# An order written out by hand for 2033 steps: its first three batches re-ordered, and the PSUM banks written down with it

## The chip, the cores and the metric

The kernel runs on one core of a Trainium2 chip. The metric is the device time of one execution in microseconds, as the median of several runs. A profile of one execution, taken by the hardware profiler, stands beside it.

## What is computed

Softmax attention with a one added to the sum of exponentials, and on its output a gate with a long convolution done by Fourier transform. Eight batches, twelve heads of 64, 448 positions, so a model width of 768.

```python
scores = q @ k.T / 8                       # 8 x 12 heads, 448 x 448
e = np.exp(scores - m)                     # m: the row's maximum
attn = e / (e.sum(-1) + np.exp(-m) + 1e-09)
x = heads_side_by_side(attn @ v)           # 8 x 448 x 768
x1, x2, x3 = split(x @ w_proj)             # 768 -> 3 x 768
conv = irfft(rfft(x2) * rfft(filter_fft))  # along the 448 positions
out = (x1 * conv * x3) @ w_out             # 768 -> 768, float32
```

## The kernel before

Two heads (a pair) are worked on together; `attention(i)` is one of the 48 pairs, and `dense(b)` the gate of one of the eight batches. All operations are written down as some 2033 steps by `add(engine, cost, ...)` of the class `Plan`: what a step needs and makes, which buffers it takes (`take`) and gives back (`give`). Some copies out of PSUM may go to either ScalarE (ACT) or VectorE (DVE); `FLIP` lists the numbers of the steps that swap engines.

`plan.ORDER` holds one key for each step. On each engine (TensorE, ACT, DVE, GpSimd called POOL, and SyncE called SP, which issues most transfers) the steps are sorted by it, and with `ORDER` set only the step at the head of each engine's list may start. So the order on an engine is fixed; a step whose operand is late holds up all that stands behind it on its engine. `Plan.run` plays the five lists against each other by modelled times, and in doing so chooses a PSUM bank for each step that takes one. The instructions are then written out in the order of that play, and on the chip they wait for each other by semaphores alone. The bank that a step got decides which earlier reader it must wait for.

PSUM has eight banks. Three kinds of user share them: "sc" (scores, pairs of banks), "op" (the output of a pair of heads, pairs of banks) and "hy" (all the dense part, single banks, at most five at once). The function `spots` chooses: the pair that has been free longest, or for "hy" a bank whose neighbour is taken, by preference.

How the batches flow:

- `staged(b)` loads q, k and v for batches 0 and 1, turns them with matmuls against the identity (L624, L637), and copies qT and kT out of PSUM (L486 on ACT, L488 on DVE). `loaded(b)` does it for later batches: loads by SP (L727 q, L747 k, L509 the rests) and by POOL (L754 v), casts on POOL (L733, L759, L771), and transposes by DMA (L694 qT, L705 kT).
- `more_tables` builds the Fourier tables: `mirror` is the matmul of L847, and `fr` is copied out by ACT (L854, L855).
- `attention(i)`: scores (L947, L952), exponentials on ACT (L966), the rest of an output (L977, 64-row tiles) and its main part (L997), the division (L1010 to L1012), and a DMA transpose of the result into xT (L1056). Before the second half of a pair may write its bank, a one-element step called `seen` (L987, `sinks`, on POOL for all pairs but batch 0's) waits for L977.
- `dense(b)`: sums and differences for the transform (`u`, `w`, `xf`, L1125 to L1134), the projection of x2 (L1175) with a copy out and a DMA transpose (L1188), the forward transform Z (L1223) with the filter (L1241), the gate matmuls G (L1273) with x1's copy and the product g (L1288), the inverse I (L1319), y (L1361), and the output projection (L1091). Its copy into `osb` (L486 or L488) is stored by SP (L1406). `osb` is a ring of three buffers.
- `wout_load` (L929) loads w_out by POOL's queue. It is needed by the first L1091.

The work of two or three batches overlaps: while TensorE does the scores of one batch, it does the dense part of the batch before.

An output tile's copy takes one of the three buffers, and its store gives it back:

```python
add("ACT", 0.38, w, ..., alt=None if keep else ("DVE", 0.47), need=[("O", b, st, ch)] + past("ACT"),
    make=[("os", b, st)] + [("os", b, st, ch)], take=held, give=[hy], keep=keep)
...
add("SP", 0.5, w, lambda: store(st), need=[("os", b, st)] + past("SP"), make=[("store", b, st)], give=held, ...)
```

Of the kernel before, what the change touches and what calls it, by code (L numbers as in the profile page):

```python
# [41 lines left out]
class Plan:  # L42
# [17 lines left out]
    FLIP = ()  # L60
    FETCH = (4.6, 256, 150)
# [14 lines left out]
    def __init__(self, rings):  # L76
        self.size = rings
        self.tasks = []
        self.banks = {}
        self.kept = []  # L80
        self.open = []

    def add(self, eng, cost, want, emit, need=(), make=(), take=(), give=(), dma=0.0, run=256, n=1, after=0.0, begun=(), late=0.0, turn=False, part=None, keep=False, port=False, mode=None, alt=None, mm=None):
        if alt:
            own = (eng, cost)
            (eng, cost), alt = (alt, own) if len(self.tasks) in self.FLIP else (own, alt)
            emit = lambda f=emit, e=eng: f(e)
        want = self.ORDER[len(self.tasks)] if self.ORDER else want + self.SHIFT.get(part, 0.0)
        self.tasks.append((want, len(self.tasks), eng, cost, emit, need, make, take, give, dma, after, run, n, begun, late, turn, keep, port or eng == "POOL" and not dma, mode or ("full" if eng == "PE" and not keep else None), alt, 2 * (mm or max(1, round(cost / 0.17)) if eng == "PE" and cost else 0)))

    def run(self):
# [79 lines left out]
        def spots(t):  # L171

            found, count = {}, {}
            for r, tok in t[7]:
# [47 lines left out]
        while any(queue.values()):  # L222
            moved = False
            for e in queue:
# [22 lines left out]
                if t[20]:  # L247
# [3 lines left out]
                    while edge <= fed + t[20]:  # L251
                        at = now + cost * (edge - fed) / t[20] + wait
# [1425 lines left out]
```

## Time and profile before

| | before |
|---|---|
| median of 3 runs | 373.16 us (373.08 to 374.23) |
| span of the profiled execution | 370.8 us |
| instructions | 10707 |
| TensorE (PE) busy | 356.4 us, 96% |
| VectorE (DVE) busy | 274.8 us, 74% |
| ScalarE (ACT) busy | 237.5 us, 64% |
| GpSimd (POOL) busy | 127.6 us, 34% |
| read from and written to HBM | 43.86 MB and 11.01 MB |

How to read it: the profile follows one execution, and its span goes from the first instruction to the last; the profiled execution has no time of its own beside its span, and the times of the runs are longer by what lies around it (373.16 - 370.8 = 2.36 us for the median). Busy time counts what an engine works; weight loads for TensorE (PEld) overlap its matmuls. A row of the timeline has its start, its duration, the engine, the line, the operation, the tiles out and in, and in brackets the idle time of the engine ahead of it with what ended that. SPq is SP's own queue of transfers to issue; the landing of a transfer comes later than its issue. A wait row has the engine and what waited, what it waited for, then the sum, the count and the longest, in us.

### The profile page before, as it was taken

What the parts mean: (1) busy time and instruction counts of PE and PEld (TensorE: products, weight loads), DVE (VectorE), ACT (ScalarE), POOL (GpSimd) and SP (SyncE); (2) the same over time, 40 slices, a digit from 0 to 9 for tenths busy, and PEclk for the clock granted to TensorE, in tenths of its full rate; (3) what the DMA queues carried; (4) which work ended last, traced back from release to release, by engine and by line L of the source; (5) the groups of instructions that cost most, each with busy time, mean ns of one, the idle gap of its engine ahead of it and who ended that gap; (6) DMA issues with size and microseconds to landing.
All of it is one profiled execution on the core that took longest, in us unless ns stands there. A gap on an engine that the chain in (4) does not pass through costs nothing. (4 is left out here: it accounts for less than half of the span.)

```text
span 370.8 us, 10707 instructions
## 1 busy us (share of the span) xinstructions
PE 356.4 (96%) x4300; PEld 211.8 (57%) x4300; DVE 274.8 (74%) x674; ACT 237.5 (64%) x379; POOL 127.6 (34%) x278
## 2 busy tenths in 40 slices
PE   7989999999999979999999999999999999999995
PEld 7666675554555545565555646665565655555552
DVE  5468659982789726897579977689459898779970
ACT  4999876756767548567565657867776561334343
POOL 9984251444625274265537523313100100000000
PEclk9999999999999999999999999999999999999999
DMA  9999999988999999999998799995830074125035
GB/s 169 194 191 204 207 207 205 206 169 160 168 242 156 229 214 208 235 242 192 206 182 202 166 245 192 262 208 122 171 72 1 7 196 89 42 45 170 4 129 172
DMA packets 133958, 61.93 MB, mean 167 GB/s; under 512 B 105165, under 2 KB 130704, under 8 KB 133904
## 3 DMA queue, kind: packets, MB, share of 16 engines
q1 hardware_dynamic: 111552, 48.71, 61.6%
q0 software_dynamic: 22112, 12.26, 25.4%
q8 instruction: 34, 0.56, 0.6%
q10 hardware_dynamic: 240, 0.23, 0.2%
q14 instruction: 20, 0.16, 0.2%
HBM read 43.86 MB, written 11.01 MB: 148 GB/s over the span
## 5 line engine op out<-in xcount | busy, mean ns | idle before, releaser
L966 ACT ACTIVATE e<-psum 128x896 bf16<-128x896 f32 x144 | 126.6, 920 | 40.8 <-PE psum L947 37.3
L1273 PE MATMUL psum<-xT,wproj_bf 128*128 128x448 bf16 x576 | 121.7, 353 | 0.1
L1273 PEld LDWEIGHTS <-wproj_bf 128*128 128x128 bf16 x576 | 53.4, 98 | 47.7 <-issue 5.0
L1091 PE MATMUL psum<-wout_bf,yT 128*128 128x384 bf16 x288 | 54.7, 326 | 0.8 <-DVE g L1288 0.4
L1175 PE MATMUL psum<-xf,wproj_bf 128*128 128x452 bf16 x252 | 53.9, 357 | 0.0
L947 PE MATMUL psum<-qT,kT 64*64 64x448 bf16 x576 | 45.4, 359 | 2.5 <-DVE g L1288 0.7
L997 PEld LDWEIGHTS <-e 128*128 128x128 bf16 x1152 | 42.0, 98 | 9.6 <-issue 5.2
L997 PE MATMUL psum<-vn,e 128*128 128x65 bf16 x1152 | 46.8, 194 | 0.0
L733 POOL CAST nat<-nat 112x512 bf16<-112x512 f32 x36 | 25.4, 708 | 44.7 <-DMA nat<-in_q_dram 41.8
L1241 DVE TENSOR_TENSOR t<-xs,hrs 113x768 bf16<-113x768 bf16 (+1 forms) x64 | 36.4, 578 | 2.9 <-ACT xs L486 2.3
L1288 DVE TENSOR_TENSOR g<-x,psum 128x448 bf16<-128x448 bf16 x48 | 29.2, 616 | 12.1 <-PE psum L1273 10.9
L1091 PEld LDWEIGHTS <-yT 128*128 128x128 bf16 x288 | 26.6, 98 | 19.9 <-issue 1.8
L1175 PEld LDWEIGHTS <-wproj_bf 128*128 128x128 bf16 x252 | 23.2, 96 | 22.2 <-issue 1.1
L486 ACT CAST x<-psum 128x448 bf16<-128x448 f32 (+1 forms) x39 | 20.4, 529 | 22.6 <-PE psum L1273 14.5
L759 POOL CAST nat<-nat 128x384 bf16<-128x384 f32 x36 | 21.5, 598 | 32.2 <-DMA nat<-in_k_dram 31.9
L486 ACT COPY osb<-psum 128x384 f32<-128x384 f32 x39 | 18.2, 486 | 20.1 <-PE psum L1091 15.9
L486 ACT CAST xs<-psum 113x384 bf16<-113x384 f32 (+1 forms) x41 | 19.2, 482 | 15.1 <-PE psum L1223 14.1
L1012 DVE TENSOR_TENSOR xb<-psum,den 128x896 bf16<-128x896 f32 x24 | 26.2, 1091 | 0.8
L486 ACT CAST cr<-psum 128x452 bf16<-128x452 f32 x35 | 18.0, 539 | 11.5 <-PE psum L1319 11.0
L947 PEld LDWEIGHTS <-kT 64*64 64x64 bf16 x576 | 15.6, 105 | 17.1 <-issue 12.9
L966 ACT ACTIVATE er<-psum 128x896 bf16<-128x896 f32 x24 | 22.2, 926 | 4.3 <-PE psum L952 3.5
L987 POOL MEMSET sinks<- 1x1 bf16 x18 | 1.6, 91 | 65.6 <-PE psum L977 65.6
(143 smaller groups left out, 501.3 us busy)
## 6 DMA issues: line engine op xcount, KB each, us to landing
nat<-in_q_dram SPq DMA_DIRECT2D x37, 224.0 KB, 3.8
out_dram<-osb SPq DMA_DIRECT2D x21, 384.0 KB, 3.5
nat<-in_k_dram SPq DMA_DIRECT2D x38, 192.0 KB, 3.9
nat<-in_v_dram POOLq DMA_DIRECT2D x15, 192.0 KB, 6.3
wproj_bf<-in_moe_w_proj_dram POOLq DMA_DIRECT2D x2, 1152.0 KB, 18.1
out_dram<-osb SPq DMA_DIRECT2D x12, 192.0 KB, 2.7
ks<-in_v_dram POOLq DMA_DIRECT2D x9, 192.0 KB, 4.9
rests<-in_k_dram SPq DMA_DIRECT2D x32, 48.0 KB, 4.3
```

The lines of the kernel that those rows point to most:

```text
L486: nc.scalar.copy(to, of)
L733: lambda hp=hp, qsrc=qsrc: nc.gpsimd.tensor_copy(qn[:, hp].rearrange("p j (u d) -> p u j d", u=2), qsrc.rearrange("p (u j d) -> p u j d", ...
L759: lambda hp=hp, sv=sv: nc.gpsimd.tensor_copy(kn[:, hp // 2, 3 * (hp % 2) + 1 : 3 * (hp % 2) + 4].rearrange("p j (u d) -> p u j d", u=2), sv),
L947: nc.tensor.matmul(sc[r, u, 0:S], kT[b % 2][c, hp // 2, 3 * turned + t, r], qT[b % 2][c, hp, :])
L966: nc.scalar.activation(to, of, AF.Exp, scale=SCALE)
L997: nc.tensor.matmul(out_bank(u)[:, n + 3 * turned, :], P["e"][1 + t][:, o : o + 128], vn[b % 2][:, hp, 4 * u + t, :], start=False, stop=tur ...
L1012: nc.vector.tensor_tensor(W["xb", b][:, hp // 2].rearrange("p s (u d) -> p u s d", u=2), op[:, :, :, 0:DH], rec[:].unsqueeze(3).to_broadca ...
L1091: nc.tensor.matmul(ops[:n, :DCH], y[:, dt, 0:n], wout_bf[:, dt, ch * DCH : (ch + 1) * DCH], start=(dt == 0), stop=(dt == NDT - 1),)
L1175: nc.tensor.matmul(pps, wproj_bf[:, kt, D + dt * 128 : D + (dt + 1) * 128], W["xf", b][:, :, kt, 0:FQ], start=(kt == 0), stop=(kt == NDT - 1),
L1241: nc.vector.tensor_tensor(t[:K], L["xs", par, ch][:K], h, op=ALU.mult)
L1273: nc.tensor.matmul(p[:, :S], wproj_bf[:, kt, 2 * part * D + dt * 128 : 2 * part * D + (dt + 1) * 128], xT()[:, kt, 0:S], start=(kt == 0), ...
L1288: nc.vector.tensor_tensor(g[:, dt, :], L["x1", dt], p[:, :S], op=ALU.mult)
```

## The change

Three constants change, and a few lines are added that use the new one.

- `BANK` lists a bank for each of the 535 takings of PSUM, in the order in which the steps are added; `spots` then gives that bank and no other, and the step waits in the play until it is open. 63 of the 535 differ from what the old kernel's rule had chosen (56 "hy", 7 "sc"), all within batches 0 to 2.
- `ORDER` has new keys. The resulting lists are the same as before from about TensorE's 274th of 684 steps on (ACT's 157th, DVE's 202nd, POOL's 127th, SP's 84th); ahead of that, steps stand some places earlier or later than they did.
- `FLIP` has 105 entries instead of 99; 46 copies change engine, 20 from DVE to ACT and 26 from ACT to DVE.

No operation is added or removed. Moves that the text below speaks of: on SP, the store of batch 0's tile 1 from place 64 to 52, of tile 0 from 54 to 57, of tile 2 from 78 to 76, and that of batch 1's tile 0 from 83 to 80; on TensorE, `mirror` (L847) from the second place to the fourth, behind the first two transposes, a Z of batch 1 (L1223) ahead of an L977 and a half of a score, and one L952 of batch 1's successor four places forward; on POOL, the load of w_out behind one value copy and one query cast, and a value load of batch 2 ahead of a key cast and a `seen`; on ACT, the copies of `fr` ahead of the first exponential; the second halves of the output projection (`project`, L1091) behind about 1.9 us of other matmuls in batch 0.

```diff
     FLIP = ()
+    BANK = ()
...
         self.open = []
+        self.mine = {}
...
+        for r, tok in take:
+            if r in self.CAP and self.BANK:
+                self.mine.setdefault((r, tok), self.BANK[len(self.mine)])
         want = self.ORDER[len(self.tasks)] if self.ORDER else want + self.SHIFT.get(part, 0.0)
...
                 open_ = [i for i in range(self.NBANKS) if i not in busy and until[i] <= now + 1e-9]
-                if r in self.PAIRS:
+                mine = self.mine.get((r, tok))
+                if mine is not None:
+                    at = (mine, mine + 1) if r in self.PAIRS else (mine,)
+                    if any(i not in open_ for i in at):
+                        return None
+                    found[(r, tok)] = at
+                elif r in self.PAIRS:
...
-    plan.ORDER = (9, 0, 6, 1370, 8, 10, 1, 5, 13, 18, 20, 11, 68, 120, 2, 14, 23, 3, 21, 19, ...
-    plan.FLIP = (30, 49, 71, 87, 94, 98, 376, 378, 380, 438, 464, 971, 975, 977, 979, 985, 993, ...
+    plan.ORDER = (4, 2, 21, 1370, 9, 11, 1, 5, 7, 18, 19, 6, 65, 75, 3, 13, 20, 0, 22, 15, ...
+    plan.BANK = (4, 7, 3, 2, 1, 6, 4, 4, 5, 7, 5, 4, 5, 2, 6, 6, 0, 1, 5, 5, 4, 0, 4, 1, ...
+    plan.FLIP = (29, 56, 75, 86, 93, 94, 97, 378, 380, 386, 437, 438, 464, 977, 981, 983, 985, ...
```

More of the change, by code (lines that the diff above doesn't have):

```diff
@@ new lines @@
+    plan.FLIP = (29, 56, 75, 86, 93, 94, 97, 378, 380, 386, 437, 438, 464, 977, 981, 983, 985, 991, 1000, 1005, 1007, 1014, 1027, 1033, 1047, 1077, 1083, 1105, 1107, 1110, 1116, 1118, 1123, 1135, 1145, 1173, 1211, 1221, 1240, 1242, 1256, 1260, 1270, 1276, 1286, 1294, 1320, 1322, 1351, 1353, 1368, 1381, 1383, 1388, 1398, 1400, 1428, 1436, 1472, 1476, 1481, 1505, 1514, 1518, 1523, 1533, 1541, 1573, 1585, 1599, 1604, 1611, 1618, 1640, 1644, 1649, 1651, 1675, 1679, 1689, 1693, 1703, 1746, 1751, 1753, 1772, 1777, 1782, 1796, 1802, 1810, 1814, 1824, 1838, 1856, 1900, 1905, 1907, 1909, 1916, 1932, 1940, 1944, 1954, 1994)
```

4 lines of the change are left out of this document (2 added, 2 removed).

## The prediction

> **What bounds the kernel now.** The page comes first, its busy rows and its slices.
>
> ```profile
> span 370.8 us, 10707 instructions
> PE 356.4 (96%) x4300; PEld 211.8 (57%) x4300; DVE 274.8 (74%) x674; ACT 237.5 (64%) x379; POOL 127.6 (34%) x278
> ...
> PEclk9999999999999999999999999999999999999999
> ```
>
> TensorE is busy for 96% of the span at the full clock (a 9 is 90% or more in every slice). The change removes no work, so all that it can win on TensorE is idle time: 370.8 - 356.4 = 14.4 us. Second, the windows say where that lies (columns: stretch, its length, busy us of each engine, granted clock, DMA share).
>
> ```profile
> 0.00:30.00 30.00, 25.59 (x513) 19.41 (x514) 18.20 (x52) 24.24 (x36) 27.38 (x68) 1.00 1.26 185
> 30.00:60.00 30.00, 29.95 (x420) 20.03 (x417) 21.64 (x56) 24.52 (x43) 11.17 (x22) 1.00 1.27 205
> 60.00:100.00 40.00, 39.14 (x484) 21.86 (x483) 28.63 (x69) 26.96 (x43) 17.74 (x37) 1.00 1.00 185
> 100.00:145.00 45.00, 41.19 (x529) 23.52 (x530) 31.40 (x74) 29.41 (x44) 20.64 (x49) 1.00 1.17 201
> 145.00:250.00 105.00, 104.64 (x1269) 60.57 (x1262) 84.51 (x202) 70.59 (x110) 44.12 (x88) 1.00 1.06 213
> 250.00:371.00 121.00, 115.93 (x1109) 66.42 (x1107) 90.39 (x226) 61.83 (x107) 6.60 (x17) 1.00 0.38 94
> ```
>
> Idle TensorE is 4.41 us before 30, 0.05 to 60, 0.86 to 100, 3.81 to 145, 0.36 to 250 and 5.07 after. The new ORDER equals the old one from about 145 us on (TensorE's place 274 of 684), so the 5.43 us behind that stay, and 9.13 us are in play. A microsecond won ahead of 145 passes to the end, if nothing between 145 and 250, where TensorE never rests, is pinned to a transfer.
>
> Third, TensorE's waits by releaser.
>
> ```profile
> PE psum L977 <- DVE osb L488: 2.5, 2, 2.3
> ...
> PE psum L1223 <- DMA x<-ldm: 0.8, 1, 0.8
> ...
> PE psum L947 <- DVE g L1288: 0.7, 2, 0.5
> ...
> PE psum L1319 <- DVE x L488: 0.4, 1, 0.4
> ...
> PE psum L1091 <- DVE yT L1361: 0.3, 1, 0.3
> ```
>
> The first is one hold-up in two pieces, larger than any other. The timeline shows it.
>
> ```profile
> 95.15 0.48 ACT L486 COPY osb<-psum 128x384 f32<-128x384 f32 x1 [1.50 <-PE psum L1091]
> ...
> 109.81 0.47 SPq L1406 DMA_DIRECT2D out_dram<-osb  x1
> ...
> 124.72 0.41 SPq L1406 DMA_DIRECT2D out_dram<-osb  x1
> ...
> 127.12 0.48 ACT L486 COPY osb<-psum 128x384 f32<-128x384 f32 x1 [1.66 <-PE psum L1091]
> ...
> 131.66 1.02 DVE L488 COPY osb<-psum 128x384 f32<-128x384 f32 x2 [3.81 <-DMA out_dram<-osb]
> 132.27 0.19 PE L977 MATMUL psum<-vn,er 64*64 64x65 bf16 x1 [2.25 <-DVE osb L488]
> ...
> 132.73 0.29 PE L977 MATMUL psum<-vn,er 64*64 64x65 bf16 x13 [0.28 <-DVE osb L488]
> ...
> DMA to landing us min/median/max: 4.3/5.6/6.8
> ...
> out_dram<-osb SPq DMA_DIRECT2D x21, 384.0 KB, 3.5
> ```
>
> Output tiles go through osb, a ring of three. Batch 0's tile 1 was in osb at 95.63, but its store stands far back in SP's queue, at 124.72, and lands 6.8 us later, about 131.5 (the row of landings is that of these two stores; the last is of all 21 whole tiles). VectorE's copy of batch 1's next tile needs that buffer, stands 3.81 us with all of VectorE's queue behind it, and holds a PSUM bank. TensorE's next operation in line, the rest of an attention head's output (L977), needs that bank: 2.25 + 0.28 = 2.53 us.
>
> **The change, part by part.** I sum against the profiled 370.8 us of span; the median run is 373.16, so 2.36 us lie outside the span, and I take them as unchanged.
>
> *The store.* In the new ORDER the store of batch 0's tile 1 goes from SP's place 64 to 52, that of tile 0 from 54 to 57. Place 52 was at about 109 in the old run, place 57 about 115.5 (old first store: place 54 at 109.81). Even at 6.8 us both land by 122.5, 4.6 us ahead of the ACT copy at 127.12 that opens batch 1's output. So the 3.81 us on VectorE go, and with them TensorE's 2.53: **-2.5 us**. What is late next at that place is the head's own exponentials; L977's operands were there (nothing else is named), so I take no rest. Bounds: -2.5 and 0, the latter if another bank holder takes over.
>
> *The start.* ACT is the bound of 10 to 30.
>
> ```profile
> 10.00:30.00 20.00, 17.73 (x418) 12.62 (x419) 12.24 (x29) 18.96 (x29) 18.10 (x38) 1.00 1.38 193
> ...
> 6.16 0.35 PE L847 MATMUL psum<-ft,jm 113*113 113x452 bf16 x1 [0.62 <-DVE ft L870]
> ...
> 8.74 1.73 ACT L966 ACTIVATE e<-psum 128x896 bf16<-128x896 f32 x2 [0.68 <-PE psum L947]
> ...
> 10.36 0.54 ACT L854 CAST fr<-psum 113x452 bf16<-113x452 f32 x1
> ...
> 10.93 0.36 ACT L855 ACTIVATE fr<-psum 113x226 bf16<-113x226 f32 x1
> ```
>
> ACT has 1.04 us free of 20 there. The change sends the mirror matmul (L847) behind the first transposes, so its 0.62 us stands where nothing waits, and the two fr copies (0.90 us) ahead of the first exponential, in an ACT that is idle then. It also moves copies of qT and kT between ACT and DVE; a pair costs as much as it frees. At best -0.62 and -0.90 are one gain seen on two engines, so -0.9; at worst the fr copies delay the first exponential by what they take, +0.9. I take **-0.5**: the idle 0.68 us ahead of 8.74 covers most of the copies, but not all.
>
> *Small stalls to 145.* 0.4 (L1319), 0.3 (L1091) and 0.5 (the longest at L947) wait for VectorE. Second halves of project move about 1.9 us of matmul later, and the gate g ahead of L947 stands two long VectorE operations earlier with its x1 copy on ACT. All of it would be -1.2; I take half, **-0.6**: of the copies that change engine, 26 go to VectorE and 20 to ACT, and VectorE, for which these stalls wait, gets six more at about 0.5 us (two took 1.02 at 131.66). These 3 us are hidden, as a sum, by the 45 us that it stands idle in the four windows to 145; where one of them lies ahead of a g, they aren't.
>
> *Tile modes.* TensorE changes between 64-row and 128-row tiles 168 times instead of 164. The nearest row is an exposed weight load:
>
> ```profile
> L1273 PEld LDWEIGHTS <-wproj_bf 128*128 128x128 bf16 x576 | 53.4, 98 | 47.7 <-issue 5.0
> ```
>
> Four times 98 ns is **+0.4**, between 0 and that.
>
> *Banks.* BANK fixes by hand the bank that the planner had chosen by rule; 63 of 535 differ, all in the first three batches. It adds no instruction. A worse bank would be a wait of a matmul for a copy; the single waits quoted above (0.3 to 0.5) bound one such. At nothing: of the eight banks the dense part may hold five, and an idle one covers a worse choice; without that cover it is one such wait.
>
> *Waits that the change adds.* Rows of the four places where a moved step stands close to its operand:
>
> ```profile
> 54.21 0.83 POOL L929 DMA_DIRECT2D wout_bf<-in_moe_w_out_dram  x1
> ...
> 59.16 0.61 POOL L733 CAST nat<-nat 112x512 bf16<-112x512 f32 x1 [1.86 <-DMA nat<-in_q_dram]
> ...
> DMA to landing us min/median/max: 11.9/11.9/11.9
> ...
> 74.13 2.42 PE L1091 MATMUL psum<-wout_bf,yT 128*128 128x384 bf16 x12
> ...
> 95.21 1.84 SPq L1188 DMA_TRANSPOSE x<-ldm  x1
> ...
> 102.98 0.53 PE L1223 MATMUL psum<-x,ft 113*113 113x384 bf16 x2 [0.81 <-DMA x<-ldm]
> ...
> 121.55 1.93 SPq L705 DMA_TRANSPOSE kT<-nat  x1
> ...
> 127.02 0.38 PE L952 MATMUL psum<-qT,kT 64*64 64x448 bf16 x4
> ...
> 161.07 0.97 POOL L733 CAST nat<-nat 112x512 bf16<-112x512 f32 x1 [6.22 <-DMA nat<-in_q_dram]
> ...
> 162.76 0.09 POOL L987 MEMSET sinks<- 1x1 bf16 x1
> ...
> 163.19 0.31 PE L977 MATMUL psum<-vn,er 64*64 64x65 bf16 x14
> ```
>
> (1) The w_out load goes behind a value copy and the query cast at 59.16 in POOL's queue, so it is issued at 59.8 (59.16 + 0.61) or somewhat later instead of 54.21. At 11.9 us it lands near 72, and its first matmul stood at 74.13: the margin falls from 8.0 us to about 2, less what the start wins. (2) Z of batch 1 (L1223) goes ahead of an attention head's rest, while x2's transpose of 95.21 landed at 102.98: it is pinned there. What is won before 100 (0.5 + 0.4) can be lost in this wait, and the two operations moved behind it (0.45 us) no longer cover it. (3) The score matmul of 127.02 goes four places earlier, to about 124.7; its kT, issued at 121.55, lands a few us later. The transpose keeps place 61 in SP's queue: the store and two loads are new ahead of it, three loads go behind it. (4) A value load on POOL moves ahead of a key cast and of a sinks, which releases an L977 of batch 1. Each is worth 0 to about 1.5 us; I take **+0.7** for all, mostly (2).
>
> **Sum:** -2.5 - 0.5 - 0.6 + 0.4 + 0.7 = -2.5 us, so 373.16 - 2.5 = **370.6 us**.
>
> **The rivals.** *The gain is taken back behind the change* (within 0.3%). L977 at 163.19 comes 0.34 us behind POOL's sinks (162.76 + 0.09), which stands behind two casts that waited 6.22 us for a query load. If that load keeps its time, TensorE can be no more than 0.34 us earlier there, and the time is 372.8. For it: SP issues almost without a break from 132 to 160, and sends the load by its own pace. Against it: before that stretch SP waits for POOL casts of loads that the late store delayed, and the store is gone from there.
>
> *The moved store takes the loads' bandwidth* (within 0.3%). 384 KB at the 201 GB/s of 100 to 145 are 1.96 us. If these bytes go ahead of the transposes that now run with the store behind them, the score matmul of (3) stands for about 2 us, and -2.5 becomes -0.5: 372.6. For it: the later store took 6.8 us against 4.3, so they do meet something. Against it: a store only changes its place among the same bytes, and 127.02 lay some 2 us behind its kT, if a transpose lands in the 3.5 us that a store's median takes (121.55 + 3.5 = 125.05). A rule of the Trainium skill speaks for this rival (*DMA: Bandwidth & Descriptors*, "Queues, rings and completion order"): a DMA engine takes turns between the rows of queues packet by packet, and transfers of one issuer need not complete in the order of issue. By it the early store would slow its neighbours rather than wait for its turn, and the sum would be nearer to -0.5; the trace agrees only in that two equal stores took 4.3 and 6.8 us.
>
> *A new wait is larger than the old* (slower). The w_out load: its place in POOL's queue is behind a cast that waits for a query load. That wait was 1.86 us at 59.16, but such a wait reached 6.22 us at 161.07. With 6.22 the load is issued near 64.2 and lands at 76.1, and any transfer ahead of it pushes it on; TensorE then stands 2 us at 74. From a landing at 76.6 on, 2.5 behind 74.1, the kernel is slower than before; at 78 it is 374.6. For it: a margin of about 2. Against it: the cast's load is issued by SP before it, at about the old time.
>
> *All stalls ahead of 145 go* (faster still): 2.53 + 1.2 + 0.81 + 0.9 = 5.4 us, 367.7. For it: the change touches each of these places. Against it: (1) to (4).
>
> *The bound is not the store.* If the buffer that batch 1's copy needs were another one than the early store frees, as copies are re-ordered too, only the rest is left, -0.5 - 0.6 + 0.4 + 0.7 = 0: no change. Against it: the order of the first copies into osb in batch 1 still meets tiles 1, 0, 2 in turn.
>
> **How the numbers follow.** A difference under 0.3%, 1.1 us, can't be told from none here. My case (-1.2 to -4) has 0.52 and its own range is 369.2 to 372.0; all stalls 0.12; together faster 0.64. Taken back behind the change 0.13, the store's bytes 0.05, not the store 0.03: the same 0.21. A new wait: slower 0.15. The range for 8 in 10 leaves out part of either end: it goes from 367.7, the all-gone sum, to 374.3, a new wait of 3.6 us against 2.5 won.
>
> **What would show it.** Right: no copy into osb that waits for a store, L977 without its 2.25, the window 100 to 145 with 2 us or less of idle TensorE, and 145 to 250 still with about 0.4. Wrong by the first rival: 145 to 250 shows some 2 us idle, at L977 behind POOL's sinks, or at a score matmul for a transpose. By the second: L1091 near 74 waits for a transfer of wout_bf, or L1223 for x2 by more than 0.8. By the start: the first exponential after 8.74. The forecast falls if TensorE's idle time from 0 to 145 is not some 2 us under the old 9.13.

## The result, and the profile after

The changed kernel takes 377.51 us in the median (376.8 to 380.43) against 373.12 us (371.81 to 374.23) of the old one beside it: 1.0144 times as long, with an interval of 1.0095 to 1.0193. It is slower by 1.4%, and lies above the range (367.7 to 374.3) as well. Ratios in this document compare executions that lie within 1.5% of their kernel's fastest; five of twelve of a_v24, four of eight of a_storeback and five of seven of b_sppool lie outside. The profiled execution took 376.8 us with a span of 375.0, 4.2 us over the old span, so the two traces show about the whole difference.

The page of the changed kernel, busy rows and clock. Its lines are those of the old kernel plus 12 behind L468 (L947 is now L959, L977 is L989, L1319 is L1331).

```profile
span 375.0 us, 10781 instructions
PE 358.1 (95%) x4329; PEld 213.7 (57%) x4329; DVE 283.4 (76%) x680; ACT 235.1 (63%) x373; POOL 129.2 (34%) x278
PEclk9999999999999999999999999999999999999999
```

TensorE has 29 matmuls more (4329 against 4300). The listed work is the same; the extra ones are idle matmuls (76 now, 47 before), which the plan itself puts into gaps of its play to keep TensorE's clock up. "No operation is added" was true of the lists alone. Of the 1.7 us by which TensorE is busier, 1.2 are theirs (5.8 us against 4.6); the other 2.5 us of the longer span are idle time (375.0 - 358.1 = 16.9 us against 14.4). The windows, as before:

```profile
0.00:30.00 30.00, 25.63 (x511) 20.29 (x512) 16.77 (x50) 23.52 (x35) 24.82 (x62) 1.00 1.25 187
30.00:60.00 30.00, 30.00 (x446) 20.16 (x443) 22.46 (x58) 23.30 (x41) 11.10 (x23) 1.00 1.12 191
60.00:100.00 40.00, 36.90 (x451) 21.01 (x451) 31.14 (x71) 23.69 (x36) 17.92 (x36) 1.00 1.11 186
100.00:145.00 45.00, 42.56 (x540) 23.84 (x537) 35.73 (x77) 30.29 (x45) 18.84 (x41) 1.00 1.06 188
145.00:250.00 105.00, 103.31 (x1234) 59.52 (x1232) 83.53 (x196) 69.87 (x110) 49.07 (x100) 1.00 1.11 217
```

TensorE's idle time to 145 is 4.37 + 0 + 3.10 + 2.44 = 9.91 us, where the forecast needed some 2 us under the old 9.13. The stretch 100 to 145, with the store, did win (3.81 to 2.44); 60 to 100 lost 2.24 (0.86 to 3.10), and 145 to 250 lost 1.33. TensorE's waits by releaser:

```profile
PE psum L1331 <- DVE yh L1259: 2.7, 1, 2.7
PE psum L959 <- DMA kT<-nat: 2.2, 2, 1.2
PE psum L989 <- POOL sinks L999: 1.5, 1, 1.5
...
PE psum L1235 <- DMA x<-ldm: 0.3, 1, 0.3
```

The wait of L977 for osb (2.5) is gone, and new ones have come: the inverse transform for VectorE's sum yh, scores for a key transpose (in two places), and a head's rest for POOL's `sinks`. In the timeline:

```profile
60.46 0.90 POOL L783 COPY vn<-nat 128x192 bf16<-128x192 bf16 x2 [3.63 <-DMA nat<-in_v_dram]
61.31 1.67 POOL L745 CAST nat<-nat 112x512 bf16<-112x512 f32 x1
62.93 0.83 POOL L941 DMA_DIRECT2D wout_bf<-in_moe_w_out_dram  x1
63.75 0.62 POOL L771 CAST nat<-nat 128x384 bf16<-128x384 f32 x1
63.94 2.82 DVE L1259 TENSOR_TENSOR yh<-t 112x384 bf16<-112x384 bf16 x2
...
65.80 0.75 POOL L783 COPY vn<-nat 128x192 bf16<-128x192 bf16 x2
66.82 0.28 PE L1331 MATMUL psum<-bt,yh 112*128 112x113 bf16 x2 [2.69 <-DVE yh L1259]
...
110.36 0.57 PE L959 MATMUL psum<-qT,kT 64*64 64x448 bf16 x8 [0.93 <-DMA kT<-nat]
...
122.09 0.75 POOL L783 COPY vn<-nat 128x192 bf16<-128x192 bf16 x2 [3.52 <-DMA nat<-in_v_dram]
122.79 0.50 POOL L771 CAST nat<-nat 128x384 bf16<-128x384 f32 x1
123.23 0.09 POOL L999 MEMSET sinks<- 1x1 bf16 x1
123.38 0.31 PE L989 MATMUL psum<-vn,er 64*64 64x65 bf16 x14 [1.52 <-POOL sinks L999]
...
147.93 0.38 PE L959 MATMUL psum<-qT,kT 64*64 64x448 bf16 x4 [1.24 <-DMA kT<-nat]
```

POOL stands 3.63 us for a value load, and what has gathered behind that copy then runs without a gap to 66.5. In that run one of the two sums yh takes 2.40 us by its own record (median 0.35). The groups by form show the same: these 32 sums take 445 ns in the mean against 377 in the old kernel.

```profile
L1259 DVE TENSOR_TENSOR yh<-t 112x384 bf16<-112x384 bf16 x32 | 13.8, 445 | 0.2
```

TensorE pays 2.69 us for it. At 110 it waits 0.93 us for a key transpose. At 122 it is the same pattern on POOL, and `sinks`, which stands behind the copy and a key cast, costs 1.52. The key transpose behind 147.93 went from SP's place 69 to 73 and was issued 11 us later (143.59 against 132.40).

The table follows TensorE: when a step starts in the old trace, and how much later (+) or earlier the same step starts in other traces. The two columns "again" are a second profile of either kernel; the last four are experiments told below. An entry is one trace and not a median.

| step at | old trace | after | after again | before again | b_store | h_start | a_sppool | b_sppool |
|---|---|---|---|---|---|---|---|---|
| rest of pair 7 | 40.96 | +0.95 | +1.46 | +0.69 | +0.17 | +0.92 | +0.92 | +1.99 |
| score of pair 11 | 58.62 | +0.99 | +1.51 | +0.81 | +0.21 | +1.08 | +0.97 | +2.10 |
| score of pair 13 | 73.83 | +3.95 | +5.06 | +1.07 | +0.36 | +0.47 | +1.59 | +2.54 |
| score of pair 17 | 98.62 | +3.40 | +4.64 | +0.98 | +0.28 | +0.45 | +0.84 | +5.75 |
| output 0 of batch 1 | 125.30 | +4.98 | +6.33 | +2.51 | +0.17 | -0.21 | +0.37 | +7.07 |
| behind the osb stall | 134.13 | +1.88 | +3.68 | +0.77 | -2.40 | -2.80 | -2.30 | +4.51 |
| score of pair 24 | 144.73 | +3.20 | +5.00 | +0.77 | -2.40 | -2.80 | -2.29 | +5.58 |
| projection, batch 4 | 209.81 | +3.93 | +7.19 | +0.76 | -1.14 | -2.83 | -1.78 | +7.09 |
| last output | 362.47 | +4.25 | +7.44 | +0.75 | -1.15 | -2.84 | -2.06 | +7.09 |

The start costs about 1 us and the inverse about 3. The key transpose at 110 and `sinks` cost 1.6 more by 125. Between 125 and 134, where the old trace has its stall, 3.1 come back, and the key transpose at 147.9 takes 1.3 of them again.

### The profile page after: what moved, and what is told of

The parts are those of the page before. It is cut to its first block, busy times and chain, and to the rows that moved or that the text cites. A ratio compares the mean times of both kernels' runs of the same rounds, so it can differ in the third digit from the quotient of the medians.

```text
span 375.0 us, 10781 instructions
## 1 busy us (share of the span) xinstructions
PE 358.1 (95%) x4329; PEld 213.7 (57%) x4329; DVE 283.4 (76%) x680; ACT 235.1 (63%) x373; POOL 129.2 (34%) x278
## 5 line engine op out<-in xcount | busy, mean ns | idle before, releaser
L1285 PE MATMUL psum<-xT,wproj_bf 128*128 128x448 bf16 x576 | 121.7, 353 | 0.4 <-DVE g L1300 0.4
L1285 PEld LDWEIGHTS <-wproj_bf 128*128 128x128 bf16 x576 | 53.4, 98 | 48.3 <-issue 5.7
L1103 PE MATMUL psum<-wout_bf,yT 128*128 128x384 bf16 x288 | 54.4, 326 | 0.1
L959 PE MATMUL psum<-qT,kT 64*64 64x448 bf16 x576 | 45.7, 360 | 4.3 <-DMA kT<-nat 2.2
L1253 DVE TENSOR_TENSOR t<-xs,hrs 113x768 bf16<-113x768 bf16 (+1 forms) x64 | 38.2, 608 | 1.1 <-ACT xs L498 0.6
L1103 PEld LDWEIGHTS <-yT 128*128 128x128 bf16 x288 | 26.7, 97 | 17.9 <-issue 1.1
L959 PEld LDWEIGHTS <-kT 64*64 64x64 bf16 x576 | 15.6, 105 | 20.8 <-issue 14.7
L498 ACT CAST xs<-psum 113x384 bf16<-113x384 f32 (+1 forms) x39 | 18.3, 481 | 13.7 <-PE psum L1235 13.5
L1259 DVE TENSOR_TENSOR yh<-t 113x384 bf16<-113x384 bf16 (+1 forms) x64 | 25.9, 421 | 0.5
```

Of the source, the lines that this page charges most:

```text
L498: nc.scalar.copy(to, of)
L959: nc.tensor.matmul(sc[r, u, 0:S], kT[b % 2][c, hp // 2, 3 * turned + t, r], qT[b % 2][c, hp, :])
L1103: nc.tensor.matmul(ops[:n, :DCH], y[:, dt, 0:n], wout_bf[:, dt, ch * DCH : (ch + 1) * DCH], start=(dt == 0), stop=(dt == NDT - 1),)
L1253: nc.vector.tensor_tensor(t[:K], L["xs", par, ch][:K], h, op=ALU.mult)
L1259: nc.vector.tensor_tensor(yh[:K, par, n, ch * DCH : (ch + 1) * DCH], t[:K, 0, :], t[:K, 1, :], op=(ALU.subtract, ALU.add)[n],)
L1285: nc.tensor.matmul(p[:, :S], wproj_bf[:, kt, 2 * part * D + dt * 128 : 2 * part * D + (dt + 1) * 128], xT()[:, kt, 0:S], start=(kt == 0), ...
```

## The experiments

Two theories stood. *Feed*: the new lists of SP and POOL, which load, cast and turn the operands of the coming batches, run behind from 42 us on, and TensorE meets them late in several places. *Start*: the new start, with 76 idle matmuls in place of 47, puts TensorE 1 us behind, and the rest follows from that. Beside them stood the question of what the store was worth at all. Where `MOVE` appears, it gives a step (by number) another key in ORDER, which puts it elsewhere on its own engine and nothing else.

### Both kernels again

**before_again** and **after_again** are the two kernels unchanged.

> The kernel before, unchanged, profiled a second time. If the stall is the kernel's own: TensorE waits 2 to 2.6 us at L977 near 132 for the copy into osb again, and VectorE 3 to 4 us for the store. If it was the one execution's: the store that is issued near 125 lands in 4 to 5.5 us, VectorE waits 0 to 1.5 us, TensorE less than 1 us; then the term of 2.5 us was read from a chance landing, and the early store could never give more than a part of it in the median. The ratio shows what no change looks like: 1.000 within 0.003.

> The changed kernel, unchanged, profiled a second time. If its waits are the lists' own: TensorE waits for a key transpose or at the inverse between 62 and 85 us, for the one-element step near 123 and for a key transpose near 147 again, 6 us or more in all, though of other sizes. If they were the one execution's: these waits are gone and others stand elsewhere. Ratio 1.012 to 1.018.

Measured: 0.9993 (0.9965 to 1.002) and 1.0188 (1.0158 to 1.0218). The timeline of the old kernel's second profile, store and copies of batch 1's first output:

```profile
125.86 0.41 SPq L1406 DMA_DIRECT2D out_dram<-osb  x1
129.63 0.48 ACT L486 COPY osb<-psum 128x384 f32<-128x384 f32 x1 [1.65 <-PE psum L1091]
131.73 1.02 DVE L488 COPY osb<-psum 128x384 f32<-128x384 f32 x2
```

The landings of batch 0's first two stores there, and TensorE's largest waits:

```profile
DMA to landing us min/median/max: 3.6/4.0/4.4
```

```profile
PE psum L1223 <- DMA x<-ldm: 2.0, 1, 2.0
PE psum L947 <- DVE xb L1012: 1.8, 3, 1.0
```

The copy at 131.73 waits for nothing: this store landed 3.6 us after its issue, not 6.8. L977 does not stand, and yet the span is 371.5 us and TensorE is idle for 3.78 us from 100 to 145, as in the first profile (3.81): here x2 came 2.0 us late instead. The osb stall that the forecast was built on stood in one of the two profiles. The table shows a second reason beside the landing: TensorE comes 2.51 us later to this place and leaves it only 0.77 later. At 131.73 even the landing of the first profile, near 131.5, would have been in time.

In the second profile of the changed kernel its waits come again:

```profile
PE psum L959 <- DMA kT<-nat: 3.0, 2, 1.7
PE psum L1331 <- DVE yh L1259: 2.4, 1, 2.4
...
PE psum L1235 <- DMA x<-ldm: 1.0, 1, 1.0
...
PE psum L989 <- POOL sinks L999: 0.8, 1, 0.8
```

So these waits belong to the changed kernel, and not to one execution.

### The store

**b_store**: the old kernel, with batch 0's tile 1 stored early (SP's place 52).

```diff
# old kernel
+    MOVE = {1084: 619}     # step 1084 is the store of batch 0's tile 1
+    plan.ORDER = tuple(MOVE.get(i, k) for i, k in enumerate(plan.ORDER))
```

> The kernel before, with one step moved: the store of batch 0's tile 1 from place 64 to 52 in SP's queue. Theory of the prediction: this is worth the whole old stall, TensorE's 2.53 us at L977 near 132 and VectorE's 3.81 us go, and the kernel gains 2.0 to 2.5 us against before (0.6%). Rival, taken back: the stall goes, but the rest of a head's output near 163, behind POOL's casts of a query load, holds TensorE until its old time, and the kernel gains 0.4 us. Rival, the store's 384 KB slow the transposes of keys behind it, and a score matmul between 115 and 127 waits for them: no gain.

Measured: 0.999 (0.9967 to 1.0014), no difference. Its trace has the gain and a part of its return: -2.40 us at 134, -1.86 at 166, -1.14 at 210. Where a first part of the return, 0.44 us, is lost:

```profile
160.16 0.61 POOL L733 CAST nat<-nat 112x512 bf16<-112x512 f32 x1 [7.36 <-DMA nat<-in_q_dram]
160.72 0.50 POOL L759 CAST nat<-nat 128x384 bf16<-128x384 f32 x1
161.16 0.09 POOL L987 MEMSET sinks<- 1x1 bf16 x1
...
161.31 0.31 PE L977 MATMUL psum<-vn,er 64*64 64x65 bf16 x14 [0.44 <-POOL sinks L987]
```

It is the very `sinks` of the first rival, behind a longer wait for the query load (7.36 us against 6.22). The next part, 0.7 us, is not: near 176 a projection (L1175) waits for ACT's copy into ldm.

**a_storeback**: the changed kernel, with that store put back (`MOVE = {1084: 744}`).

> The changed kernel, with the store of batch 0's tile 1 back in its old place in SP's queue, behind the key and query loads. Theory of the prediction: this one move is worth the old stall, so VectorE's copy into osb waits for the store again, TensorE's L989 stands some 1.5 to 2.5 us near 135, and the time is 1 to 2.5 us longer: 378.5 to 380. Rival, the early store's bytes delay the transposes of keys behind it and take as much as they give: no change, 377.5. Rival, TensorE is now so late there (4 to 5 us) that the store has landed anyhow in either place: no change and no wait for osb.

Measured: 1.0105 (1.0054 to 1.0156), which can't be told from the changed kernel's 1.0144. Its profiled execution is long (383.61 us), with a wait of 6.0 us for a key transpose; no copy into osb waits for the store in it, as the third expectation has it.

**c_bank1**: the old lists, no `BANK`, but the one osb tile whose copy held up L977 gets bank 3, so that the head's pair of banks is another.

```diff
# old kernel, with the change's lines that give a listed bank, but no BANK
+    plan.mine.update({('hy', ('O', 1, 1, 0)): 3})
```

> The kernel before, with one bank written down: the copy of batch 1's tile 1 (first half), which waits for the store in VectorE's queue, holds bank 3 instead of 6; the rule then gives the head's output of L977 the pair 0 and 1 instead of 6 and 7. Lists, engines and the late store are those of before. Theory: TensorE's 2.53 us hang on the bank and not on the store; VectorE still waits for the store near 130, TensorE does not, and it is 2 to 2.5 us earlier at 134. Of that 1 to 1.5 us reach the end (the early store alone kept 1.15 of 2.40 in its trace): 371 to 372.5. Rival: VectorE's queue behind the waiting copy holds TensorE at its next need instead (a sum on VectorE, the gate), and the time stays within 0.5 us of before.

Measured: 1.0016 (0.9987 to 1.0045). In its trace L977 doesn't stand, but the store landed 3.8 us after its issue, so the stall would have been absent with the old bank too: inconclusive on the bank, and one more execution in which the store is harmless.

### Which lists

**h_start**: the old kernel, in which only what stood ahead of about 42 us takes the new order and the new engines (84 steps of TensorE, 45 of POOL, 10 of SP, 111 of ACT and VectorE); banks by the rule. **h_rest** is its counterpart: old up to there, new behind.

```diff
# old kernel
-    plan.ORDER = (9, 0, 6, 1370, 8, 10, ...       # all old
+    plan.ORDER = (4, 2, 21, 4370, 9, 11, ...      # h_start: new keys for the steps ahead of 42 us, old sequence behind; FLIP likewise
```

> The kernel before, with the new order and engines up to about 42 us alone (TensorE's first 84 steps, POOL's 45, SP's 10, ACT's and VectorE's first 111 together), banks by the old rule. The trace of the changed kernel is 0.95 us late at 41 us. If the start's loss is its own: TensorE is 0.7 to 1.1 us late at 42 here, nothing behind needs to pay more, and the kernel is 0.7 to 1.1 us slower than before. Rival, hidden: the lateness is absorbed by 75 us, where the old kernel waits for VectorE anyhow, and the time is that of before. Rival, banks: with banks by the rule the start is not late, and what the trace shows comes from BANK.

> The new order and engines from about 42 us on alone, with the old ones ahead of that, banks by the old rule. If parts add up, this is the changed kernel's loss without the start's: slower than before by 2.5 to 4.5 us, with waits at the inverse near 63, for a key transpose between 75 and 85 (0 to 9 us, by how the load of w_out meets the transposes in that execution), for the one-element step near 122 and for the key transpose near 146. Rival, banks: without BANK these waits are gone and the kernel is not slower than before.

Measured: h_start 0.9957 (0.9933 to 0.9981), faster than the old kernel; h_rest 1.0139 (1.0105 to 1.0174), as slow as the whole change. So the loss sits behind 42 us. h_start has 67 idle matmuls and is 0.92 us late at 41, as the changed kernel is (0.95), and yet it ends first: with the old lists behind it, that microsecond is gone by 118 (-0.27). That speaks against *Start*.

**a_sppool** is the changed kernel with the old lists of SP and POOL behind 42 us (SP's places 13 to 83, POOL's 45 to 126); **b_sppool** is the old kernel with the new ones.

```diff
# changed kernel
-    plan.ORDER = (... new keys of SP 13-83 and POOL 45-126 ...)
+    plan.ORDER = (... keys that give these steps their old sequence ...)
```

> The changed kernel, with SP's and POOL's lists from about 42 us on as they were before; TensorE, ACT, VectorE, the start and BANK stay changed. The early stores go back too. Theory: the loss is in the order of loads, casts and transposes. Then the waits of the inverse near 64, of the score for a key transpose (75 to 85, and near 147) and of a head's rest for the one-element step near 123 go, and the time is that of before or up to 2 us less, 371 to 373.5. Rival: TensorE's steps were moved too close to their operands (scores 3.6 us earlier near 74), so the same waits come with the old lists as well, and the time stays above 376.

> The kernel before, with SP's and POOL's lists from about 42 us on as in the changed kernel, the early stores among them; TensorE, ACT, VectorE, start and banks as before. Theory: the loss is in the order of loads, casts and transposes, so this alone is 3 to 6 us slower than before, with waits for a key transpose and for the one-element step. Rival, TensorE's steps: with the old order of TensorE the operands are in time, and the early store makes it up to 2 us faster. If both this kernel and its complement are slow, the lists and TensorE's order fit only together.

| | all else old | all else new |
|---|---|---|
| SP and POOL old behind 42 us | 1 | a_sppool 1.0023 (0.9992 to 1.0054) |
| SP and POOL new behind 42 us | b_sppool 1.0448 (1.0405 to 1.0491) | the change 1.0144 (1.0095 to 1.0193) |

The two lists decide whether there is a loss, whatever the rest is. The executions of b_sppool spread from 379.71 to 508.42 us, and the shortest, which is the profiled one, is 1.020 of the old kernel's median beside it (372.26); the table gives its direction, not its size. It has waits for key transposes (1.8 us) and for `sinks` (1.4) with all else old. In the trace of a_sppool none of the new waits is left, and there is no osb stall although its stores are the late ones: TensorE makes up 2.67 us between 125 and 134 there, nearly the changed kernel's 3.1. A window in which TensorE does the same in both kernels shows the feed running behind ahead of any stall: 30 to 58 us, first the changed kernel, then a_sppool.

```profile
30.00:58.00 28.00, 28.00 (x428) 19.33 (x425) 20.46 (x53) 22.63 (x39) 11.10 (x23) 1.00 1.10 191
```

```profile
30.00:58.00 28.00, 28.00 (x428) 19.33 (x425) 20.64 (x53) 22.63 (x39) 12.85 (x26) 1.00 1.26 200
```

TensorE and ACT are alike; POOL has done 23 operations instead of 26, the DMA share is 1.10 instead of 1.26. The old kernel has a DMA share of 1.28 there, h_start 1.27, b_sppool 1.06. (The operations compare only between kernels with one start: the old kernel, whose POOL did more ahead of 30, has 21, and b_sppool 19.) By 145 us POOL has worked 72.68 us in the changed kernel, against 76.93 in the old one.

The traces also show where the two lists part first. These are POOL's first operations behind 42 us, in the changed kernel and then in a_sppool:

```profile
52.32 0.61 POOL L745 CAST nat<-nat 112x512 bf16<-112x512 f32 x1 [9.68 <-DMA nat<-in_q_dram]
...
55.56 0.76 POOL L766 DMA_DIRECT2D nat<-in_v_dram  x1
```

```profile
49.58 0.51 POOL L526 CAST nat<-rests 64x384 bf16<-64x384 f32 x1 [7.31 <-issue]
50.21 0.61 POOL L745 CAST nat<-nat 112x512 bf16<-112x512 f32 x1
50.77 0.76 POOL L766 DMA_DIRECT2D nat<-in_v_dram  x1
```

The new list puts a query cast first, and POOL stands 9.68 us for its load. What stands behind it comes later: the issue of a value load by 4.8 us, SP's first query transpose at 53.39 instead of 50.85, and w_out's load, which the new list also moves, at 62.93 instead of 53.96. In all eleven traces with the new lists this first cast stands 8.2 to 11.0 us and the value load is issued between 55.1 and 56.8; in all eight with the old lists, the value load is issued between 49.3 and 51.8. No experiment moved this cast alone, so whether it is the move that matters isn't shown.

**h_start_store** adds the early store to h_start.

> The kernel before with the new start up to 42 us and the store of batch 0's tile 1 moved early. If the two gains are separate, 1.6 us and 0.5 us add up to about 2.1 us less than before, 370.3. If both are the same stall at 132, which the banks that follow from the new start remove already, the early store adds nothing: 371, as with the start alone. If the early store harms the loads near 110, 372 or more.

Measured: 0.9983 (0.9953 to 1.0013). It adds nothing to h_start.

**a_nobank** is the changed kernel without its banks.

```diff
# changed kernel
-    plan.BANK = (4, 7, 3, 2, 1, 6, 4, ...
+    plan.BANK = ()
```

> The changed kernel without BANK: the same lists and engines, the banks chosen by the old rule. The prediction took the banks at nothing: within 1 us of the changed kernel, 376.5 to 378.5. Rival, the banks are at fault: 2 us or more faster, with the wait of the early scores for ACT's reading of their banks shorter and the start less than 0.95 us late at 41 us. Rival, the banks help: 2 us or more slower.

Measured: 1.0237 (1.0199 to 1.0275): the banks cost nothing, and with this order they may help, by up to 0.9% (against 1.0144; against 1.0188, the change's second figure, the intervals overlap).

### Single places

**b_wout**: the old kernel with w_out's load behind the query cast, as in the change (`MOVE = {364: 410.5}`). **a_wout** and **a_wearly** are the changed kernel with that load further ahead on POOL (`{364: 340}`, ahead of the value copy that waits 3.63 us; `{364: 285}`, earlier still).

> The kernel before, with one step moved: the load of w_out on POOL behind the query cast of 59.16, five places later, near its place in the changed kernel. Theory of the shared engines: its 1152 KB then run at the same time as the transposes of keys and queries that the score matmuls near 74 to 78 need, which land 5 us or more later, and TensorE waits 1 to 9 us for a key transpose near 75 to 80; the kernel is 2 us or more slower than before and its runs spread. The prediction's price, the landing of w_out itself: it lands near 72 to 74, and the kernel is within 1 us of before. Rival, the order of loads on SP in the changed kernel is what matters and not w_out: no change.

> The changed kernel, with the load of w_out back in its old place on POOL, ahead of the value copy and the query cast that it was moved behind. Theory of the crowd on POOL: in the changed kernel POOL stands for a value load, then runs a query cast, the issue of w_out and six casts and copies without a gap from 61.3 to 66.5, and VectorE's yh of 63.94, with two inputs in SBUF, takes 2.40 us instead of 0.35 because it finds no gap; with the issue taken out ahead, the casts come as their loads land, yh takes under 1 us and TensorE's wait of 2.7 us at the inverse goes: about 375. Rival, what slows yh is the transfer of w_out itself or the wait for its landing (the prediction's price): then a stall of the same size comes wherever the transfer is, and the time stays at 377.5; a stall at the first output projection would show the landing. Rival, POOL's order is not to blame but its late loads: the crowd stays without the issue, yh stays over 1.5 us, and the gain is under 1 us.

> The changed kernel, with the load of w_out on POOL nine places earlier, ahead of the query cast of pair 13, issued near 43 us, where POOL stands for loads. Theory of the meeting: the transfer is over before the key transposes of 62 to 77 us, TensorE's waits at the inverse near 64 and for the key transpose near 78 go, and the kernel is 2 to 4 us faster than the changed one: 373.5 to 375.5, the rest being the one-element step near 123 and the key transpose near 147. Rival: it delays the loads of queries and keys of 41 to 54 us by as much, and the stall moves to the scores near 60 to 65: no gain or a loss.

Measured: b_wout 0.9979 (0.9952 to 1.0005), so the place of that load costs nothing by itself. a_wout 1.0168 (1.0116 to 1.0219) and a_wearly 1.0183 (1.0129 to 1.0237): not better than the change. In a_wout the sum yh isn't late any more, and these waits stand instead:

```profile
PE psum L1235 <- DMA x<-ldm: 3.7, 2, 2.7
PE psum L959 <- DMA kT<-nat: 3.3, 2, 2.8
PE psum L989 <- POOL sinks L999: 2.9, 1, 2.9
```

**a_v24** puts the value copy ahead of `sinks` behind it (`MOVE = {203: 692}`); **a_mend** does that, the early w_out and one more (a key transpose on SP ahead of one of x2; `{364: 285, 203: 692, 201: 768}`).

> The changed kernel, with the copy of one value tile of batch 2 on POOL put behind the key cast and the one-element step that it was moved ahead of. Theory of the queue on POOL: that copy waits 3.5 us for its load (to 122.1) with the one-element step behind it, so TensorE's rest of a head's output stands 1.5 us at 123.4; put behind, this wait goes and the kernel gains up to 1.5 us, 376.0, unless the score matmul at 147.9, pinned to the transpose of its keys, takes it back: then the wait there grows from 1.24 to about 2.7 us and the time stays at 377.5. Rival, the wait is TensorE's own lateness: the one-element step is no earlier, no change.

> The changed kernel, with three moves put right: w_out's load early as in the run beside it, the value copy of batch 2 behind the one-element step, and the key transpose of pair 26 ahead of the transpose of x2 that it was put behind. Theory: these three are the loss, and with them gone the kernel is as fast as before or faster, 371 to 373.5. Rival: SP and POOL have no room left, and each mended wait comes back as another one behind it (the x2 transpose near 157): 375 or more.

Measured: a_v24 1.0089 (1.0054 to 1.0124), a_mend 1.0184 (1.0144 to 1.0224). In both the wait at 123 is gone. In a_v24 half or so of the loss may be mended (its interval overlaps with the change's), and x2 waits 1.8 us in its place; in a_mend a query transpose waits 2.2 and another `sinks` 1.5. Where one wait is mended another stands; that fits a feed that is behind as a whole.

**a_fill4** lets no gap have more than four idle matmuls.

```diff
# changed kernel, where the plan lists its idle matmuls
-        return {n: f for n, f in full.items() if f[1] > 1}
+        return {n: [f[0], min(f[1], 4)] for n, f in full.items() if f[1] > 1}
```

> The changed kernel, with at most four idle matmuls in each of the early gaps (76 in all before this edit, 17 of them in one gap; 40 now). Theory of the idle matmuls: the play of the new order sees longer gaps than the chip has, and the 17 in the gap ahead of the turned rests of k stand in TensorE's way until 12.5 us; without them that step starts near 11.8, the score behind it 0.7 us earlier, ScalarE's gap of 0.8 us at 13.4 closes, and the kernel gains 0.6 to 0.9 us: about 376.7. Rival, the fr copies alone delay the first exponential (9.28 against 8.74) and that is the whole loss of the start: no gain, 377.5, and the gap at 13.4 stays. Rival, the idle matmuls keep the clock up: the granted clock in 10 to 30 falls below 1.0 and matmuls get longer, slower by 1 us or more.

Measured: 1.0205 (1.0162 to 1.0249). Scores (L964) that start at 13.80 us in the changed kernel and at 13.36 in the old one start at 12.68 here, so the idle matmuls do hold TensorE up there. The time isn't shorter, which speaks against *Start* once more. Its profiled execution shows one wait that outweighs all else; first the wait, then two groups of the transfers from 52 to 88 us (KB each where the view has it, median us from issue to landing):

```profile
PE psum L959 <- DMA kT<-nat: 11.4, 2, 9.2
```

```profile
wout_bf<-in_moe_w_out_dram POOLq DMA_DIRECT2D x1, 1152.0 KB, 22.5
...
xT<-xb SPq DMA_TRANSPOSE x2, 12.2
```

The two rows were 12.6 and 7.4 in the changed kernel. A kernel whose feed is behind has no margin for such a collision of w_out's load with transposes; what made it so large here was not tried by itself.

**port** computes nothing of the reference (its output is zeros): it measures VectorE's operations on 128 x 384 tiles alone and beside POOL casts, to see whether a run of casts holds them up.

> None of the gate or the attention is in it, and the output is zeros: it measures what POOL's casts do to one VectorE operation. In each trial POOL runs 0, 1, 2, 4 or 6 casts of 128x384 from float32 to bfloat16 without a gap, and VectorE, a copy from PSUM later, either adds two bfloat16 tiles in SBUF (113x384), or copies from PSUM, or scales one bfloat16 tile in SBUF (128x384). Theory of the crowd on POOL: the add takes 0.35 us with no cast and is held until the run of casts ends, so that it grows by about 0.5 us with each further cast (some 2 us at 6), while the copy from PSUM stays the same. Rival, sharing: the add takes at most twice its time whatever the run's length. Rival, no hold at all: 0.35 us everywhere, and the 2.40 us of the changed kernel's trace came from something else.

Measured: sums of two SBUF tiles took 0.34 to 0.35 us alone and 0.34 to 0.63 beside casts; copies out of PSUM 0.54 to 0.56 in either case; five of six scalings of a bf16 tile 0.24 to 0.26, and the sixth, beside casts, 2.16:

```profile
20.19 2.32 POOL L79 CAST dst<-src 128x384 bf16<-128x384 f32 x5
20.46 2.16 DVE L86 TENSOR_SCALAR yt<-xa 128x384 bf16<-128x384 bf16 x1
```

A run of POOL operations can hold a VectorE operation to the end of the run; the sum itself was not held for a run here, only by one cast. The trials overlapped, so the runs were not as long as they were written.

## Why the prediction was wrong

**The store, -2.5 us: the term that was mis-sized.** What it describes did happen: no copy into osb waits, and TensorE makes up 3.1 us between 125 and 134. But a_sppool, whose stores are late, makes up 2.67 there too. The 2.53 us were one execution's, with a landing of 6.8 us; in the second profile the store landed in 3.6 and there was no stall at about the same total. By itself the early store gives 0.999 (0.9967 to 1.0014), where 2.5 us of 373 would be 0.993. The first rival (taken back behind 145, at `sinks`) came out in part in b_store's trace: 0.44 of the 1.26 us that it loses again are lost at the place that was named.

**Waits that the change adds, +0.7 us: the step that failed.** The four new waits are 2.69 + 0.93 + 1.52 + 1.24 = 6.38 us. With the start's 0.95 and without the old stall's 2.53 that makes 4.8 us; the trace's 4.25 is less, mostly because x2 costs 0.3 in place of 0.8. Of the four places that were costed, only (4), POOL's value step (a copy, not a load) ahead of `sinks`, was a price, 1.52 us, at the end of its own bound. (1), w_out's landing, came to nothing, and (2), Z's wait for x2, on which most of the 0.7 rested, to less than before; the key transposes that were late are not that of (3). The largest, the sum yh, was on no list, since I followed moved steps to their own operands. I did not ask what a POOL queue that is let loose behind a long wait does to VectorE, nor summed up whether SP and POOL as a whole still run as far ahead as before. The rows that I read said which single operand had little margin, and not that. The runs put the loss there: with the old lists of SP and POOL the time is 1.0023 of the old kernel's, with the new ones it is longer whatever the rest.

**The start, -0.5 us.** In the trace it is +0.95 at 41 us. The first exponential came at 9.28 instead of 8.74, which is within the +0.9 allowed for the two fr copies. The idle matmuls, 76 instead of 47, I did not count at all. Yet h_start, with the same order and engines at the start, ends faster (0.9957): the microsecond is absorbed in waits further on, and TensorE then runs without the stalls. So the sign was right for the time by luck, and not for the reason given; what in h_start's order wins it stays open.

**Banks at nothing.** No harm came from them; by a_nobank they may save up to 0.9%.

**Small stalls, -0.6 us, and tile modes, +0.4 us.** The three small stalls that were named (0.4, 0.3 and 0.5) are gone and one of 0.41 has come, L1285 for g at 71.14, so in this trace the term was about right. The tile modes were not tried by themselves, and their price was a mean duration of weight loads, which overlap matmuls: no run shows it.

**The rival on the other side** (a new wait larger than the old) had the direction, and a chance of 0.15. Its mechanism, w_out landing too late for L1091, did not occur: the output projection (L1091, now L1103) never waits for w_out in the changed kernel. (The forecast lists that sign under the second rival; it belongs to this one.)

What stays open is which of the moves on SP and POOL sets the feed back. Five kernels that moved one to three steps of the changed one did not mend it whole (the best, a_v24, stands at 1.0089), but none of them moved the query cast at 52.32; the sum of the two lists alone is shown. The lowest ratio measured is h_start's, and h_start_store can't be told from it.

## What to carry to other kernels

Before a stall is turned into a term of a sum, look at it in a second execution: a wait for a transfer moves with the landing (6.8 us, then 3.6 us, here for one and the same store), and another wait can fill its place at the same total. When the lists of the engines that feed a saturated one are re-ordered, first compare how far ahead those engines are in a window where the saturated one does the same work: here a DMA share of 1.10 against 1.26, and POOL's 23 operations against 26 behind the same start, told of the loss before any stall did. And if several stalls appear at once in unlike places, put back the whole list first: mending them one by one left other stalls here.

## What the runs showed of the hardware

A VectorE sum of two SBUF tiles took 2.40 us instead of 0.35 while POOL ran casts and copies without a gap, 1.95 in the second profile, and a scaling 2.16 us across five casts. In the `port` run sums beside casts took at most 0.63, so this does not come every time. The Trainium skill (*SBUF — State Buffer*, "Who interferes with whom") says that a VectorE operation with two inputs in SBUF contends with a POOL operation that reads SBUF, that their shared pair of ports is an exclusive lock, and that whoever issues first holds it for the whole instruction while the other one blocks. The traces agree that it blocks; by that rule alone the wait would end with the one instruction that holds the lock, 0.5 to 0.8 us here, and in these executions it lasted for a run of several.

The same 1152 KB load took 11.9 us in the old kernel and 22.5 beside slow transposes in a_fill4.

In eight of the nineteen traces of whole kernels TensorE's granted clock fell to 0.50 around a stall. In the second profile of the changed kernel, around the wait of 2.35 us that ends at 67.0:

```profile
66.00:68.00 2.00, 1.00 (x16) 1.01 (x17) 2.00 (x3) 0.00 (x0) 1.14 (x3) 0.74 0.94 115
68.00:70.00 2.00, 2.00 (x27) 1.78 (x25) 1.60 (x4) 0.80 (x2) 0.00 (x0) 0.50 1.06 174
```

There the second profile's TensorE lies 0.18 us behind the first at the end of this wait (67.00 against 66.82) and 1.11 behind at the score of pair 13. In the first profile the clock stayed at 1.00 behind a wait of 2.69. In a_mend it fell around one of 2.18, and in a_wout it stayed at 1.00 behind one of 2.77. In a_fill4, behind 9.15 us, it was 0.50 from 82 to 91. So a stall can cost more than its own length, and whether a short one does differs from one execution to the next.
